# Last stage of a fused attention and MLP kernel: weight sums in the middle of Strassen groups, one set of closing products in each, and a weight split a step earlier

## Chip, cores and metric

One core of a Trainium2 chip runs the whole program. The metric is device time in microseconds (us) from start to end; the kernel before was run three times. The engines named below are TensorE (PE in the rows), VectorE (DVE), ScalarE (ACT), GpSimd (POOL) and SyncE (SP), which only issues transfers here. Each engine works through its own queue in order.

## What is computed

Attention with a window of 16 and block summaries gives x, 1536 tokens by 512. Two MLPs follow; the second is the stage of this change:

```python
def _moe_ref(x, w_in, w_out):
    h = x @ w_in
    g = h - np.tanh(h)
    return (g @ w_out).astype(np.float32)

def _moe2_ref(x, w1, w2, w3, w_out):        # d_model 512, d_ff 1024
    a = x @ w1
    b = x @ w2
    h = a * b @ w3
    return (h @ w_out).astype(np.float32)
```

All is float32.

## The kernel before

**Split arithmetic.** Each float32 operand of a matmul is held as a high part (a rounded copy, made by ScalarE) and a low part (the operand less its high part, one subtraction on GpSimd, in places on VectorE). `split_mm` (lines 185 to 188) issues three matmuls of 128x128 by 128x512: high with high, then the two mixed ones. All three add into one PSUM bank of 128x512. A matmul needs the high parts, and one of each three needs the low part of the operand that comes last.

**Stages.** The first stage is attention; beside it the product w3 w_out is formed and kept as eight tiles w34[m], so that the second MLP's last two products become one. The second stage is the first MLP. The last stage, from about 392 us of the span, is the second MLP. Its tokens are three blocks of 512 (k = 0, 1, 2), its hidden width eight chunks of 128 (m = 0 to 7).

*Block 0, steps 1 to 7* (lines 740 to 768). Step m forms a = x w1 of chunk m (`product_a`, copied by ScalarE), b = x w2 (`half`), multiplies them on VectorE (`product_b`), splits the product c into `gh_c` and `gl_c`, and then runs `final` for the chunk before: four token tiles of 128, three matmuls each, c of chunk m-1 times w34[m-1], into four banks `o`. Twelve matmuls of `final` are called a set here. `w34_split(m-1)`, ScalarE's cast `w34h` and GpSimd's subtraction `w34l`, stands in step m behind `product_a`. VectorE also decodes the weights still missing (`dec`) and, in step 4, forms sums of x (`x_sums`); in step 5 these are split (`x_split`: four casts on ScalarE, four subtractions `xl` and `t` on GpSimd).

*Blocks 1 and 2: Strassen groups* (lines 788 to 810). For a pair of chunks (m, m+1; m = 0, 2, 4, 6) and the two blocks, a group of seven products replaces eight: one group for w1, one for w2. Each product is six matmuls (`seventh`). Products 6, 5, 7 and 3 use sums of weights: `w_sums` adds high and low parts of two weight tiles (`t_w`, two full-width operations), forms two tiles `s_w` of sums (four half-width ones), all on VectorE, and then splits both on ScalarE and GpSimd. In the rows `p_w` is the bank of a product, and `t`, `xh` and `xl` are parts of x.

`group` (lines 714 to 738) is a generator. The order of its products is p1, p6, p5, p7, p2, p4, p3. Four banks take them in turn, so p2, p4 and p3 take the banks of p1, p6 and p5. ScalarE copies p1 to c11; VectorE adds the others:

```python
            tt(c21, c11, add, product(6))
            p5 = product(5)
            tt(c12, c21, add, p5)
            between()
            tt(c21, c21, add, product(7))
            tt(c22, c21, add, p5)
            yield
```

`between()` (lines 775 to 777) runs the next set of `todo`, if there is one. The w1 group's results are called `sq_a` (c11, one tile for all pairs), `a` and `ab`; the w2 group's `u_b`, `b` and `ab`. Each w2 result is multiplied into its w1 partner as soon as it is complete. `split_c` then splits the four products: those of block 1 go to `todo`, those of block 2 to `last`. The places of the weight sums: the w2 sums are made after p4 of the w1 group, the next pair's w1 sums after p4 of the w2 group, the first w1 sums at the end of step 7. Between the w1 and the w2 group `between()` is called a second time. Each pair uses up two sets of `todo`, both before its w2 group; the first pair has one.

*Closing* (lines 811 to 816). The two remaining sets of `todo`, then block 2: for each token tile j the eight chunks of `last`, three matmuls each, and the copy and the transfer out.

The order of the code is the order of each queue. Space for split weights is a list `wt.free` of places, taken from its front.

Of the kernel before, what the change touches and what calls it, by code (L numbers as in the profile page):

```python
# [19 lines left out]
P = 128  # L20
# [17 lines left out]
NM = FF2 // P  # L38
TB = 512
# [6 lines left out]
NRAW = 4  # L46
# [9 lines left out]
def fused_kernel(tc, qT, kT, vN, vW, w_in, w_out, w1, w2, w3, wo2, out):  # L56
# [128 lines left out]
    def split_mm(acc, lh, ll, rh, rl, start, stop):  # L185
        mm(out=acc, lhsT=lh, rhs=rh, start=start, stop=False)  # L186
        mm(out=acc, lhsT=lh, rhs=rl, start=False, stop=False)  # L187
        mm(out=acc, lhsT=ll, rhs=rh, start=False, stop=stop)  # L188

    def low_part(eng, out, x, high):  # L190
        eng.tensor_tensor(out=out, in0=x, in1=high.bitcast(F32), op=ALU.subtract)  # L191
# [3 lines left out]
    with tc.tile_pool(name="base", bufs=1) as base, \  # L195
# [304 lines left out]
        def bank(i, name):  # L500
            return psp.tile([P, TB], F32, tag=f"b{i}", name=name)
# [82 lines left out]
        def half(z, m, k):  # L584
            nonlocal n_ab
            ph = bank(ab[n_ab % len(ab)], f"{z}_{m}_{k}")
            n_ab += 1
            columns(ph, wt.need((z, m)), k)
            return ph
# [27 lines left out]
        for n in range(NS + LAG):  # L617
            nxt = hidden(n) if n < NS else None
            if n == NS:
                a = product_a(0, 0)  # L620
            if n == NS + 1:
                pb = half("w2", 0, 0)
            wt.start()
            if n == NS + 1:
                prev = 0, 0, product_b(0, 0, a, pb)
            wt.high()
            closing = len(evac)
            evacuate()
            cur = curve(n, nxt, cur)
            wt.low()  # L630
            if not closing:
                resplit(2)
            if n >= LAG:
                back(n - LAG)
# [10 lines left out]
        def final(m, k, c, js=range(TB // P)):  # L645
            ch, cl = c
            for j in js:
                if m == 0:
                    acc[j] = bank(outs[j], f"o_{k}_{j}")
                s = slice(j * P, (j + 1) * P)  # L650
                split_mm(acc[j], ch[:, s], cl[:, s], w34p[m][0], w34p[m][1], start=m == 0, stop=m == NM - 1)
                if m < NM - 1:
                    continue
                o = tmp(("u", "u", "gh", "gl")[j], f"out_{k}_{j}", LAG + (j > 1))
                w = DM // 2 if k == NTB - 1 and j == TB // P - 1 else DM
                for i in range(0, DM, w):
                    if j % 2 and i == 0:
                        nc.scalar.copy(out=o[:, i:i + w], in_=acc[j][:, i:i + w])
                    else:
                        nc.vector.tensor_copy(out=o[:, i:i + w], in_=acc[j][:, i:i + w])  # L660
                    nc.sync.dma_start(out=out[k * TB + j * P:k * TB + (j + 1) * P, i:i + w], in_=o[:, i:i + w])

        H = KC // 2
# [2 lines left out]
        def tt(out, in0, op, in1):  # L666
            nc.vector.tensor_tensor(out=out, in0=in0, in1=in1, op=op)  # L667

        rhs = {}

        def x_sums(c):

# [7 lines left out]
                rhs[i, c] = xh[k][:, r * H + c, :], xl[k][:, r * H + c, :], t  # L680
            rhs[6, c] = t2[0][:, :], t2[1][:, :], b22

        def x_split(i, c):
            h, l, t = rhs[i, c]
            nc.scalar.copy(out=h, in_=t)
            low_part(nc.gpsimd, l, t, h)

        def w_sums(z, m):

# [24 lines left out]
        def group(z, m, lhs, c11, c12, c21, c22):  # L714

            def product(i):
                nonlocal n_ab
                acc = bank(ab[n_ab % 4], f"p{i}_{z}_{m}")
                n_ab += 1
                seventh(acc, lhs, i)  # L720
                return acc

            nc.scalar.copy(out=c11, in_=product(1))
            tt(c21, c11, add, product(6))
            p5 = product(5)
            tt(c12, c21, add, p5)
            between()
            tt(c21, c21, add, product(7))
            tt(c22, c21, add, p5)
            yield  # L730
            tt(c11, c11, add, product(2))
            yield
            tt(c21, c21, sub, product(4))
            yield
            tt(c12, c12, add, product(3))
            wt.free.extend(lhs["places"])
            wt.release((z, m))
            wt.release((z, m + 1))

        a11 = tmp("sq", "a11")  # L740
        for m in range(1, NM):
            wt.high()
            wt.low()
            wt.start(min(2, len(wt.free) - (1 if m > 5 else (7 - m) // 2)))
            a = product_a(m, 0)
            w34_split(m - 1)
            wt.unit(1)
            pb = half("w2", m, 0)
            c = product_b(m, 0, a, pb)
            wt.unit(1)  # L750
            if m == 1:
                resplit(4)
                resplit(4)
            if m == 4:
                for i in range(H):
                    x_sums(i)
            if m == 5:
                for i in (5, 6):
                    x_split(i, 0)
                    x_split(i, 1)  # L760
                wt.free += [(px, f"x{k}{c}", f"x{k}{c + 1}", 1) for k, c in ((1, 0), (2, H))]
            if m == NM - 1:
                w34_split(m)
                assert len(wt.t) == len(wt.units)
                wt.free += [(rawp, "raw", "raw", NRAW)] * NRAW
                lhs = w_sums("w1", 0)
            final(*prev)
            prev = m, 0, c
        todo, last = [(*prev, range(TB // P))], []
        for i in (7, 4):  # L770
            x_split(i, 0)
            x_split(i, 1)
        wt.free[:0] = [(px, f"x{k}{c}", f"x{k}{c + 1}", 1) for k, c in ((2, 0), (1, H))]

        def between():
# [12 lines left out]
        for m in range(0, NM, 2):  # L788
            pl_a, a12, a21 = wt.take(f"a_{m}", F32)
            pl_b, a22, b22 = wt.take(f"ab_{m}", F32)  # L790
            g = group("w1", m, lhs, a11, a12, a21, a22)
            next(g)
            next(g)
            next(g)
            lhs = w_sums("w2", m)
            next(g, None)
            between()
            pl_c, b12, b21 = wt.take(f"b_{m}", F32)
            b11 = tmp("u", f"b11_{m}")
            g = group("w2", m, lhs, b11, b12, b21, b22)  # L800
            for a, b in ((a22, b22), (a11, b11), (a21, b21)):
                next(g)
                tt(a, a, ALU.mult, b)
            if m + 2 < NM:
                lhs = w_sums("w1", m + 2)
            next(g, None)
            tt(a12, a12, ALU.mult, b12)
            todo += [split_c(a11, m, 1), split_c(a21, m + 1, 1)]
            last += [split_c(a12, m, 2), split_c(a22, m + 1, 2)]
            wt.free += [pl_a, pl_b, pl_c]  # L810
        for i in todo:
            final(*i)
        outs = [ab[(n_ab + j) % 4] for j in range(4)]
        for j in range(TB // P):
            for i in last:
                final(*i, js=(j,))


# [48 lines left out]
```

## Time and profile before

| | us |
|---|---|
| three runs | 611.51, 613.11, 613.89 |
| median | 613.11 |
| the profiled execution | 613.43 |
| its span, first to last instruction | 611.6 |
| TensorE busy | 580.0 |
| VectorE busy | 460.3 |
| ScalarE busy | 338.6 |
| GpSimd busy | 282.1 |

Busy time counts matmuls as pipelined: a matmul's duration in the rows (0.39) is longer than the step to the next one (0.23), so the step, not the duration, tells the rate. The granted clock is a share of TensorE's 2.4 GHz, and an average over the stretch where it lies between 0.5 and 1. A name in brackets behind a row is the engine and tile that ended the idle time ahead of it.

### The profile page before, as it was taken

Reading aid. Unit: us, or ns where it says so; the run is one execution under the profiler, and the core shown is the slowest. Engines: PE = TensorE matmul, PEld = TensorE weight load, DVE = VectorE, ACT = ScalarE, POOL = GpSimd, SP = SyncE. Lnnn points to the kernel's source line nnn. Section 1 sums busy time; section 2 is a strip of 40 time slices with the busy share of each in tenths; the row PEclk is TensorE's granted clock in tenths of the full one; section 3 lists DMA queues with packets and bytes.
Section 4 is the critical chain, followed back from the end, with each engine's and each line's share of the span. In section 5 each row is a group of like instructions: output and inputs, shape, how many; then the busy total and the mean of one; then the engine's idle time right before and its main releaser. Section 6 shows DMA issues by size and latency. Waiting matters only on the chain.

```text
span 611.6 us, 9059 instructions
## 1 busy us (share of the span) xinstructions
PE 580.0 (95%) x3168; PEld 463.9 (76%) x3168; DVE 460.3 (75%) x881; ACT 338.6 (55%) x741; POOL 282.1 (46%) x237
## 2 busy tenths in 40 slices
PE   8988999998999999999999999999998989898997
PEld 6666777776888888888888888877776768676786
DVE  3789987799999987589999789996535656575710
ACT  3689987777878855567766658643234121212210
POOL 3456555555465542225646226477377151515320
PEclk9989999998999999999999999999999989898999
DMA  8889996553333210023222012230000100000021
GB/s 315 316 297 306 347 308 201 170 153 98 104 103 104 103 36 0 1 69 98 81 98 70 1 34 77 96 104 0 1 0 2 69 1 1 0 1 1 1 86 53
DMA packets 19678, 59.70 MB, mean 98 GB/s; under 512 B 2096, under 2 KB 4784, under 8 KB 19632
## 3 DMA queue, kind: packets, MB, share of 16 engines
q1 hardware_dynamic: 19632, 59.12, 29.0%
q8 instruction: 25, 0.41, 0.3%
q14 instruction: 21, 0.17, 0.1%
HBM read 54.79 MB, written 3.15 MB: 95 GB/s over the span
## 4 chain that ended last, share of the span: by engine, by line
PE 65%; DVE 15%; issue 8%; POOL 7%; ACT 3%; DMA 2%; SPq 0%; POOLq 0%; DVEq 0%; ACTq 0%
PE x L187 6%; PE x L186 6%; PE x L188 6%; PE ph L187 6%; PE ph L186 6%; PE ph L188 6%; PE o L187 3%; PE o L188 3%; PE o L186 3%; PE p_w L188 3%; PE busy L403 2%; PE p_w L186 2%; PE p_w L187 2%; DVE dec L115 2%; PE s L339 2%
## 5 line engine op out<-in xcount | busy, mean ns | idle before, releaser
L150 POOL TENSOR_TENSOR wl<-dec,wh 128x512 fp32r<-128x512 f32 x72 | 111.7, 1555 | 50.7 <-ACT wh L143 42.7
L191 POOL TENSOR_TENSOR gl<-g,gh 128x512 fp32r<-128x512 f32 x48 | 65.4, 1361 | 141.0 <-ACT gh L535 80.3
L186 PE MATMUL x<-gh,wh 128*128 128x512 f32 x192 | 75.6, 394 | 1.8 <-ACT gh L535 1.8
L187 PE MATMUL x<-gl,wh 128*128 128x512 f32 x192 | 75.4, 393 | 1.0 <-POOL gl L191 1.0
L188 PE MATMUL x<-gh,wl 128*128 128x512 f32 x192 | 75.4, 392 | 0.0
L186 PE MATMUL ph<-xh,wh 128*128 128x512 f32 x192 | 74.8, 390 | 0.0
L188 PE MATMUL ph<-xh,wl 128*128 128x512 f32 x192 | 74.7, 389 | 0.0
L187 PE MATMUL ph<-xl,wh 128*128 128x512 f32 x192 | 74.7, 389 | 0.0
L115 DVE SCALAR_TENSOR_TENSOR dec<-raw,dec 128x512 uint32<-128x512 uint32 x45 | 65.4, 1454 | 1.5
L530 ACT ACTIVATE u<-ph 128x512 f32<-128x512 f32 x48 | 28.8, 600 | 53.7 <-PE ph L188 53.7
L143 ACT CAST wh<-dec 128x512 fp32r<-128x512 f32 x72 | 44.6, 623 | 15.3 <-DVE dec L115 15.3
L191 POOL TENSOR_TENSOR s_w<-s_w,s_w 128x512 fp32r<-128x512 f32 x16 | 21.6, 1372 | 64.3 <-ACT s_w L703 56.9
L703 ACT CAST s_w<-s_w 128x512 fp32r<-128x512 f32 x16 | 9.9, 621 | 73.0 <-DVE s_w L667 72.6
L540 DVE TENSOR_TENSOR g<-ph,u 128x512 f32<-128x512 f32 x48 | 32.8, 683 | 19.5 <-ACT th L531 19.4
L186 PEld LDWEIGHTS x<-gh,wh 128*128 128x128 f32 x192 | 36.3, 189 | 10.2 <-ACT gh L535 2.2
L525 DVE COPY_PREDICATED g<-mk,th 128x512 f32<-128x512 uint32 x48 | 40.9, 853 | 4.0
L353 ACT ACTIVATE pr<-pr,nm 128x120 f32<-128x120 f32 x96 | 37.0, 390 | 12.0 <-DVE nm L350 11.7
L187 PEld LDWEIGHTS x<-gl,wh 128*128 128x128 f32 x192 | 36.5, 190 | 9.0 <-POOL gl L191 1.3
L188 PEld LDWEIGHTS x<-gh,wl 128*128 128x128 f32 x192 | 36.4, 190 | 7.6
L188 PEld LDWEIGHTS ph<-xh,wl 128*128 128x128 f32 x192 | 36.1, 188 | 7.5
L186 PEld LDWEIGHTS ph<-xh,wh 128*128 128x128 f32 x192 | 36.1, 188 | 7.5
L187 PEld LDWEIGHTS ph<-xl,wh 128*128 128x128 f32 x192 | 36.0, 188 | 7.4
(153 smaller groups left out, 1458.7 us busy)
## 6 DMA issues: line engine op xcount, KB each, us to landing
raw<-w SPq DMA_DIRECT2D x32, 512.0 KB
raw<-w_in SPq DMA_DIRECT2D x16, 512.0 KB
raw<-w_out SPq DMA_DIRECT2D x16, 512.0 KB
vg<-vW SPq DMA_DIRECT2D x8, 768.0 KB
raw<-wo SPq DMA_DIRECT2D x8, 512.0 KB
kt<-kT SPq DMA_DIRECT2D x7, 544.0 KB
vn<-vN SPq DMA_DIRECT2D x8, 384.0 KB
qt<-qT SPq DMA_DIRECT2D x7, 384.0 KB
```

The lines of the kernel that those rows point to most:

```text
L115: lambda tu=tu, su=su, lo=lo: stt(out=tu, in0=lo, scalar=29, in1=su, op0=ALU.logical_shift_right, op1=ALU.bitwise_or)])
L143: nc.scalar.copy(out=h, in_=self.t[n])
L150: nc.gpsimd.tensor_tensor(out=l, in0=self.t[self.n_low], in1=h[:, :].bitcast(F32), op=ALU.subtract)
L186: mm(out=acc, lhsT=lh, rhs=rh, start=start, stop=False)
L187: mm(out=acc, lhsT=lh, rhs=rl, start=False, stop=False)
L188: mm(out=acc, lhsT=ll, rhs=rh, start=False, stop=stop)
L191: eng.tensor_tensor(out=out, in0=x, in1=high.bitcast(F32), op=ALU.subtract)
L339: mm(out=ps[r, i, :], lhsT=qt[n][r, t * QT:(t + 1) * QT], rhs=kt[n][r, t * CW:t * CW + NC], start=True, stop=True)
L353: nc.scalar.activation(out=pr[g][:, i, :], in_=pr[g][:, i, :], func=AF.Exp, scale=-1.0, bias=nm[g][:, i:i + 1], accum_out=z[g][:, i:i + 1])
L525: nc.vector.copy_predicated(out=g, mask=mask[:, :].bitcast(U32), data=t)
L530: nc.scalar.activation(out=u, in_=ph, func=AF.Square)
L540: nc.vector.tensor_tensor(out=gn, in0=ph, in1=u, op=ALU.mult)
```

## The change

Five things.

1. `group` gains a `yield` behind the sum with p5. The w2 sums are made there, in the w1 group; the next pair's w1 sums there, in the w2 group.
2. The second `between()` is gone. The set in the middle of the w2 group, which found `todo` empty before, now takes one: one set in each group. The first pair's w2 group still finds none.
3. `w34_split(m)` stands at the end of step m, ahead of `final` of the chunk before; `w34_split(0)` one step further forward, in the last step of the stage before. The number of places that `wt.start` leaves free is lowered to suit.
4. In step 5 the four subtractions of `x_split` go from GpSimd to VectorE. In step 7 the first w1 sums stand ahead of `product_a`.
5. At the end, token tile 0 of block 2 is run for six of its eight chunks ahead of the two remaining sets, in banks of its own (`spare`).

```
                 pb = half("w2", 0, 0)
+                w34_split(0)
...
-                    acc[j] = bank(outs[j], f"o_{k}_{j}")
+                    acc[k, j] = bank((outs + spare)[j + TB // P * (k == 2)], f"o_{k}_{j}")
...
-        def x_split(i, c):
+        def x_split(i, c, eng):
             h, l, t = rhs[i, c]
             nc.scalar.copy(out=h, in_=t)
-            low_part(nc.gpsimd, l, t, h)
+            low_part(eng, l, t, h)
...
             tt(c12, c21, add, p5)
+            yield
             between()
...
-            wt.start(min(2, len(wt.free) - (1 if m > 5 else (7 - m) // 2)))
+            wt.start(min(2, len(wt.free) - (1 if m > 5 else (6 - m) // 2)))
+            if m == NM - 1:
+                assert len(wt.t) == len(wt.units)
+                wt.free += [(rawp, "raw", "raw", NRAW)] * NRAW
+                lhs = w_sums("w1", 0)
             a = product_a(m, 0)
-            w34_split(m - 1)
...
-                    x_split(i, 0)
-                    x_split(i, 1)
+                    x_split(i, 0, nc.vector)
+                    x_split(i, 1, nc.vector)
...
-            if m == NM - 1:
-                w34_split(m)
-                assert len(wt.t) == len(wt.units)
-                wt.free += [(rawp, "raw", "raw", NRAW)] * NRAW
-                lhs = w_sums("w1", 0)
+            w34_split(m)
             final(*prev)
...
             next(g)
-            next(g)
-            next(g)
             lhs = w_sums("w2", m)
-            next(g, None)
-            between()
+            for _ in range(4):
+                next(g, None)
...
             g = group("w2", m, lhs, b11, b12, b21, b22)
+            next(g)
+            if m + 2 < NM:
+                lhs = w_sums("w1", m + 2)
             for a, b in ((a22, b22), (a11, b11), (a21, b21)):
                 next(g)
                 tt(a, a, ALU.mult, b)
-            if m + 2 < NM:
-                lhs = w_sums("w1", m + 2)
...
+        spare += [ab[(n_ab + j) % 4] for j in range(4)]
+        for i in last[:NM - 2]:
+            final(*i, js=(0,))
         for i in todo:
             final(*i)
-        outs = [ab[(n_ab + j) % 4] for j in range(4)]
         for j in range(TB // P):
-            for i in last:
+            for i in last[0 if j else NM - 2:]:
```

What the order of the queues shows at three places. First GpSimd in steps 4 to 6 of block 0 (`gl_c` is the low part of c, `xl` and `t` are the x splits). Before:

```order
L191 TENSOR_TENSOR w34l_4791<-w_4_113,w34h_0_4789 128x512
L191 TENSOR_TENSOR gl_c_0_4809<-u_a_0_4787,gh_c_0_4808 128x512
L191 TENSOR_TENSOR xl_122<-x2a_0_1976,xh_119 128x512
L191 TENSOR_TENSOR xl_122<-x2a_1_1977,xh_119 128x512
L191 TENSOR_TENSOR t_1_0_4755<-x2a_2_1982,t_0_0_4754 128x512
L191 TENSOR_TENSOR t_1_1_4761<-x2a_3_1983,t_0_1_4760 128x512
L191 TENSOR_TENSOR w34l_4849<-w_5_114,w34h_1_4790 128x512
```

GpSimd in the same steps, after:

```order
L191 TENSOR_TENSOR w34l_4764<-w_4_113,w34h_0_4762 128x512
L191 TENSOR_TENSOR gl_c_0_4809<-u_a_0_4792,gh_c_0_4808 128x512
L191 TENSOR_TENSOR w34l_4820<-w_5_114,w34h_1_4763 128x512
L191 TENSOR_TENSOR gl_c_0_4870<-u_a_0_4850,gh_c_0_4869 128x512
L191 TENSOR_TENSOR w34l_4875<-w_6_115,w34h_0_4873 128x512
L150 TENSOR_TENSOR wl_4891<-dec_4835,wh_4890 128x512
```

The low part of w34[5] now follows c of chunk 5 at once, and the four splits are no longer ahead of it.

Then VectorE in the w2 group of the second pair, from the sum with p5 on (bank `p_w_2_5287` before, `p_w_2_5275` after). Before:

```order
L667 TENSOR_TENSOR b_0_5268<-b_1_5269,p_w_2_5287 128x512
L667 TENSOR_TENSOR b_1_5269<-b_1_5269,p_w_2_5295 128x512
L667 TENSOR_TENSOR ab_1_5164<-b_1_5269,p_w_2_5287 128x512
L667 TENSOR_TENSOR ab_0_5163<-ab_0_5163,ab_1_5164 128x512
L667 TENSOR_TENSOR u_b_2_5270<-u_b_2_5270,p_w_2_5305 128x512
L667 TENSOR_TENSOR sq_a_4513<-sq_a_4513,u_b_2_5270 128x512
L667 TENSOR_TENSOR b_1_5269<-b_1_5269,p_w_2_5314 128x512
L667 TENSOR_TENSOR a_5162<-a_5162,b_1_5269 128x512
L667 TENSOR_TENSOR t_w_4_5323<-wh_4444,wl_4445 128x512
L667 TENSOR_TENSOR t_w_4_5324<-wh_4514,wl_4515 128x512
L667 TENSOR_TENSOR s_w_4_5325<-t_w_4_5324 128x256
```

VectorE there, after:

```order
L668 TENSOR_TENSOR b_0_5256<-b_1_5257,p_w_2_5275 128x512
L668 TENSOR_TENSOR t_w_4_5283<-wh_4444,wl_4445 128x512
L668 TENSOR_TENSOR t_w_4_5284<-wh_4519,wl_4520 128x512
L668 TENSOR_TENSOR s_w_4_5285<-t_w_4_5284 128x256
L668 TENSOR_TENSOR s_w_4_5285<-s_w_4_5285,t_w_4_5283 128x256
L668 TENSOR_TENSOR s_w_4_5286<-t_w_4_5283,t_w_4_5284 128x256
L668 TENSOR_TENSOR s_w_4_5286<-t_w_4_5283,s_w_4_5285 128x256
L668 TENSOR_TENSOR b_1_5257<-b_1_5257,p_w_2_5311 128x512
L668 TENSOR_TENSOR ab_1_5164<-b_1_5257,p_w_2_5275 128x512
```

The six weight sums move from behind the product with p4 to behind the first use of p5's bank, and ahead of its second use (`ab_1`).

Last TensorE in the same group, at the end of p5. Before:

```order
L186 MATMUL p_w_2_5287<-xh_119,s_w_2_5_0_5240 128x512
L187 MATMUL p_w_2_5287<-xl_122,s_w_2_5_0_5240 128x512
L188 MATMUL p_w_2_5287<-xh_119,s_w_2_5_1_5241 128x512
L186 MATMUL p_w_2_5295<-xh_117,s_w_2_7_0_5244 128x512
L187 MATMUL p_w_2_5295<-xl_120,s_w_2_7_0_5244 128x512
```

TensorE there, after:

```order
L188 MATMUL p_w_2_5275<-xh_119,s_w_2_5_1_5200 128x512
L186 MATMUL o_0_5207<-w34h_1_4482,gh_c_1_5151 128x512
L187 MATMUL o_0_5207<-w34l_4574,gh_c_1_5151 128x512
L188 MATMUL o_0_5207<-w34h_1_4482,gl_c_1_5152 128x512
L186 MATMUL o_1_5211<-w34h_1_4482,gh_c_1_5151 128x512
L187 MATMUL o_1_5211<-w34l_4574,gh_c_1_5151 128x512
```

A set of twelve now stands between p5 and p7 of this group; before, it stood ahead of the group's p1.

## Rows read from the trace of the kernel before

**Rows 1.** Page, busy time of TensorE: us, share of the span, instructions.
```profile
PE 580.0 (95%) x3168; PEld 463.9 (76%) x3168; DVE 460.3 (75%) x881; ACT 338.6 (55%) x741; POOL 282.1 (46%) x237
```
**Rows 2.** Waits of PE, 440 to 612: us in total, times, longest.
```profile
PE p_w L186 <- ACT s_w L703: 9.2, 5, 2.4
PE p_w L188 <- POOL s_w L191: 2.5, 4, 0.6
```
**Rows 3.** Timeline of PE, six marks: start, duration, engine, line, operation.
```profile
406.76 0.50 PE L186 MATMUL o<-w34h,gh_c 128*128 128x512 f32 x1
...
463.34 0.40 PE L186 MATMUL p_w<-xh,wh 128*128 128x512 f32 x1
...
528.30 0.40 PE L186 MATMUL o<-w34h,gh_c 128*128 128x512 f32 x1
...
549.95 0.39 PE L188 MATMUL p_w<-xh,wl 128*128 128x512 f32 x1
...
578.81 0.50 PE L186 MATMUL o<-w34h,gh_c 128*128 128x512 f32 x1
...
607.67 0.40 PE L188 MATMUL o<-w34h,c 128*128 128x512 f32 x1
```
**Rows 4.** Timeline of PE, matmuls that waited: idle before them and its releaser.
```profile
408.55 0.50 PE L187 MATMUL o<-sq_w34l,gh_c 128*128 128x512 f32 x1 [1.28 <-POOL sq_w34l L191]
...
466.30 0.51 PE L186 MATMUL p_w<-t,s_w 128*128 128x512 f32 x1 [1.42 <-ACT s_w L703]
...
552.67 0.51 PE L186 MATMUL p_w<-t,s_w 128*128 128x512 f32 x1 [2.34 <-ACT s_w L703]
...
554.03 0.58 PE L188 MATMUL p_w<-t,s_w 128*128 128x512 f32 x1 [0.62 <-POOL s_w L191]
...
580.61 0.51 PE L188 MATMUL o<-w34h,gl_c 128*128 128x512 f32 x1 [1.07 <-POOL gl_c L191]
```
**Rows 5.** Stretches: us, busy PE, PEld, DVE, ACT, POOL, granted clock, DMA, GB/s.
```profile
463.00:470.00 7.00, 4.96 (x21) 3.44 (x20) 3.23 (x4) 3.80 (x7) 5.99 (x5) 1.00 0.00 1
...
491.00:499.80 8.80, 5.77 (x18) 3.99 (x17) 5.49 (x10) 4.00 (x7) 5.92 (x5) 0.81 0.01 2
...
520.80:527.00 6.20, 3.83 (x10) 2.31 (x9) 4.46 (x8) 3.42 (x6) 3.39 (x3) 0.73 0.00 0
...
549.80:557.70 7.90, 4.94 (x14) 3.33 (x13) 4.71 (x9) 4.00 (x7) 5.00 (x4) 0.79 0.00 1
```
**Rows 6.** Timeline of DVE around the end of the third pair's w2 group.
```profile
544.93 0.69 DVE L667 TENSOR_TENSOR b<-b,p_w 128x512 f32<-128x512 f32 x1 [0.70 <-PE p_w L188]
...
549.63 0.68 DVE L667 TENSOR_TENSOR t_w<-wh,wl 128x512 f32<-128x512 f32 x1
...
552.16 0.42 DVE L667 TENSOR_TENSOR s_w<-t_w,s_w 128x256 f32<-128x256 f32 x1
552.50 0.68 DVE L667 TENSOR_TENSOR b<-b,p_w 128x512 f32<-128x512 f32 x1
553.21 1.31 DVE L667 TENSOR_TENSOR a<-a,b 128x512 f32<-128x512 f32 x1
```
**Rows 7.** Timelines of ACT and POOL at the same place.
```profile
552.00 1.29 ACT L703 CAST s_w<-s_w 128x512 fp32r<-128x512 f32 x2 [10.65 <-DVE s_w L667]
...
556.93 0.58 ACT L723 COPY sq_a<-p_w 128x512 f32<-128x512 f32 x1 [1.23 <-POOL gl_c L191]
...
552.70 2.97 POOL L191 TENSOR_TENSOR s_w<-s_w,s_w 128x512 fp32r<-128x512 f32 x2 [11.15 <-ACT s_w L703]
```
**Rows 8.** Timelines of POOL and DVE in step 7, and the first group.
```profile
462.27 1.62 POOL L191 TENSOR_TENSOR gl_c<-u_a,gh_c 128x512 fp32r<-128x512 f32 x1 [1.79 <-ACT gh_c L600]
...
468.82 5.04 POOL L191 TENSOR_TENSOR xl<-x2a,xh 128x512 fp32r<-128x512 f32 x4
...
462.78 1.39 DVE L667 TENSOR_TENSOR s_w<-t_w 128x256 f32<-128x256 f32 x1
464.21 1.39 DVE L667 TENSOR_TENSOR s_w<-s_w,t_w 128x256 f32<-128x256 f32 x1
```

More of the change, by code (lines that the diff above doesn't have):

```diff
@@ L648, in final @@
                 if m == 0:
-                    acc[j] = bank(outs[j], f"o_{k}_{j}")
+                    acc[k, j] = bank((outs + spare)[j + TB // P * (k == 2)], f"o_{k}_{j}")
                 s = slice(j * P, (j + 1) * P)
-                split_mm(acc[j], ch[:, s], cl[:, s], w34p[m][0], w34p[m][1], start=m == 0, stop=m == NM - 1)
+                split_mm(acc[k, j], ch[:, s], cl[:, s], w34p[m][0], w34p[m][1], start=m == 0, stop=m == NM - 1)
                 if m < NM - 1:
@@ L657, in final @@
                     if j % 2 and i == 0:
-                        nc.scalar.copy(out=o[:, i:i + w], in_=acc[j][:, i:i + w])
+                        nc.scalar.copy(out=o[:, i:i + w], in_=acc[k, j][:, i:i + w])
                     else:
-                        nc.vector.tensor_copy(out=o[:, i:i + w], in_=acc[j][:, i:i + w])
+                        nc.vector.tensor_copy(out=o[:, i:i + w], in_=acc[k, j][:, i:i + w])
                     nc.sync.dma_start(out=out[k * TB + j * P:k * TB + (j + 1) * P, i:i + w], in_=o[:, i:i + w])
@@ L667, in tt @@
             nc.vector.tensor_tensor(out=out, in0=in0, in1=in1, op=op)
-        rhs = {}
+        rhs, spare = {}, []
         def x_sums(c):
@@ L770, in fused_kernel @@
         for i in (7, 4):
-            x_split(i, 0)
-            x_split(i, 1)
+            x_split(i, 0, nc.gpsimd)
+            x_split(i, 1, nc.gpsimd)
         wt.free[:0] = [(px, f"x{k}{c}", f"x{k}{c + 1}", 1) for k, c in ((2, 0), (1, H))]
```

## The prediction

> **What bounds the kernel now.** The page's busy times come first: TensorE is busy 95% of the span, no other engine over 76% [rows 1], so the time is TensorE's own work plus what it waits. The view of waits, cut to the last third, names for whom: the first product that takes a sum of weights waits five times for ScalarE's high part of it, 9.2 us in all, and then four times for GpSimd's low part, 2.5 [rows 2].
>
> To price the waits I count matmuls. From the first matmul of an `o` product at 528.30 to the last of p1 at 549.95 lie 95 steps without a wait: 21.65 / 95 = 0.228 us each [rows 3]. So one Strassen product (6 matmuls) takes 1.37 and one set of w3 w_out products (12, `final` in the code) 2.73. Three stretches stand against that [rows 3]. **A**, 406.76 to 463.34, the plain steps: 228 matmuls are 52.0, measured 56.6, so 4.6 over. **B**, 463.34 to 578.81, the Strassen groups: 420 matmuls (56 products and 7 sets) are 95.7, measured 115.5, so 19.8 over. **C**, 578.81 to 607.67, the closing sets: 119 are 27.1, measured 28.9, so 1.7 over. Together 26.1.
>
> Where they sit: in A at the second matmul of a set, which needs the low part of w34 (idle 1.28 at 408.55, and four smaller or like it); in B at p6 of a w1 group (1.42 at 466.30; 2.34 and 0.62 at 552.67 and 554.03); in C once, at 580.61 [rows 4]. B's 19.8 is more than the 11.7 of idle time in [rows 2]. Three of the five waits, those before w1 groups 2, 4 and 6, are followed by a lower clock: in the stretches from 491, 520.8 and 549.8 the granted clock is 0.81, 0.73 and 0.79, a mixture of 2.4 and 1.2 GHz, which is worth at most 0.19 x 8.8, 0.27 x 6.2 and 0.21 x 7.9, each time 1.7 [rows 5]. After the shorter waits around 466.30 the clock stayed at 1.00 [rows 5].
>
> Why p6 waits: VectorE forms the six weight sums of the next w1 group only after p4 of the w2 group has been added, 549.63 to 552.50; then come ScalarE's cast (552.00) and GpSimd's low part (552.70), and TensorE has only p1 to do meanwhile [rows 6, 7].
>
> **The change part by part.**
> *Weight sums in the middle of a group.* They now stand on VectorE right behind the sum with p5. From there to the next group's p6, TensorE has a set (2.73), p7, p2, p4, p3 and p1: 2.73 + 5 x 1.37 = 9.6. The chain needs 0.7 for the p5 sum, some 2.3 until the first half is summed (549.63 to 551.9), 0.7 for the cast and 1.3 for the low part: 5.0 [rows 6, 7]. Where there is no set (the w2 group of the first pair) the cover is 6.8. All five waits at p6 go, and the low clock with them. The sums for the very first w1 group move ahead of step 7's products in the same way. Gain: B's 19.8.
>
> *w34 split a step ahead.* One cast and one subtraction move half a step forward per step; GpSimd did the subtraction behind `wl` and, in step 5, behind four splits of x sums. These four go to VectorE: 2.8 at the price of its sums, ahead of the decoding of a weight that step 7 is the first to use. The low part is then done a step before its set. Gain: A's 4.6. No DMA changes its place.
>
> *End.* Six quarter sets (18 matmuls, 4.1) of finished parts stand ahead of the sets that wait for GpSimd's last splits. Gain: about C's 1.7. The spare banks belong to p7 and its followers, read by then.
>
> So without any new wait: 613.43 (the profiled execution; the median of three is 613.11) - 26.1 = **587.3**.
>
> *What is late next.* The sums now stand ahead of VectorE's additions of p7 and of p5 into c22, and c22 is what frees p5's bank, which p3 takes. Let T be the end of p5. VectorE: sum with p5 0.7, weight sums 2.87, two dependent additions 1.4, so c22 is done at T + 5.0 [rows 6]. TensorE comes to p3 at T + 3 x 1.37 = 4.1 without a set between, at 6.8 with one.
> (a) w2 group, first pair, no set: waits 0.9, whatever else happens.
> (b) w2 groups of the other three pairs: VectorE is on time at p5, 1.8 to spare: 0.
> (c) w1 groups of pairs 2, 4, 6: VectorE is late here. From the end E of the w2 group's p3 it still has products to finish: nine operations of 0.67 (seven from 544.93 to 549.63) from p7's end, E - 4.1, are done at E + 1.9, and one or two of them stand beside a GpSimd subtraction and double (1.31 at 553.21, where a sum takes 0.68) [rows 6]: E + 3.2. Then ScalarE has two casts and the copy of p1 into `sq_a` (as at 556.93, behind GpSimd's use of that tile), about 1.8 [rows 7]; VectorE two sums, 1.4; the weight sums 2.87; two additions, 1.4: E + 10.7 with no other delay. TensorE reaches p3 at E + 4.1 + 2.7 + 4.1 = 10.9. So nothing to spare, and the four splits of c on GpSimd fall just there: one subtraction in the way is up to 1.3 more [rows 8]. I take 1.0 each for pairs 4 and 6, and 1.9 for pair 2, where (a) leaves VectorE about 0.9 later: 3.9, between 0 and 7.
> (d) w1 group, first pair: VectorE has two output copies more (1.3 at the price of sums) and GpSimd's four x splits (5.04) lie beside the weight sums [rows 8]: c22 at T + 6.3 to T + 8.4 against 6.8; I take 1.2, between 0 and 1.6.
> (e) step 7: the weight sums now stand beside three GpSimd subtractions, the third the low part of the last w2 unit, which TensorE needs 0.5 into the next product: 0.4, between 0 and 0.8.
> Sum 0.9 + 3.9 + 1.2 + 0.4 = 6.4, and 0.1 at each restart (0.5): 587.3 + 6.9 = **594.2**. Each of these waits is under 2 us, like those after which the clock stayed at 1.00, so I add nothing for it.
>
> The price of meeting GpSimd is read from step 7 of the kernel before: two half-width sums, 0.42 elsewhere, took 1.39 each, the first beside a subtraction that began at 462.27 [rows 6, 8]. The Trainium skill (SBUF — State Buffer, Who interferes with whom) states that a VectorE instruction with two SBUF inputs contends with a GpSimd one that reads SBUF, and that the later one blocks fully. By that, the sums placed in the middle of groups would meet whatever GpSimd does there, which speaks against the new place. The rows agree.
>
> **The rivals.**
> 1. *Cover holds everywhere but in (a).* For: (c) is a tie before any collision. Against: four GpSimd splits follow each pair. 587.3 + 0.9 = 588.2.
> 2. *VectorE and GpSimd meet in every group.* The weight sums then take 2.87 + 2 x 0.97 = 4.8, as in step 7 [rows 8]. Waits at p3: (a) 2.8; (c) 3.8 + 2.9 + 2.9; (d) 2.8; (b) 3 x 0.1; (e) 0.8: 16.3, so 603.6; with four waits long enough to bring the low clock, at 1.7 each, 610. The rule of the Trainium skill named above (SBUF — State Buffer, Who interferes with whom) is this rival's mechanism. Against: in the w2 groups GpSimd is idle until the sums themselves feed it.
> 3. *Slower: VectorE becomes the bound.* Place: p3 of all eight groups. Per pair VectorE has 14 sums and 4 products of 0.7 and two times 2.87, 18.3, against TensorE's 84 + 24 matmuls, 24.6. GpSimd has eight subtractions a pair of 1.26 [rows 8]; if every one blocks VectorE for its whole length that is 28.4. Over four pairs 15, and the low clock after each of eight waits, 1.7 each, 14: 587.3 + 29 = 616. It is slower than before from 26.1 / 8 = 3.3 us per group on. Against: it needs every collision, each at full length, and a wait in each group long enough for the clock.
> 4. *The split a step ahead does not come early*, since the cast still queues behind ScalarE's copies: A's 4.6 stays: 598.8. Against: the cast follows the c cast directly, and its subtraction is needed 5 us later.
>
> **How the numbers follow.** Forecast 594.2: 0.58. Rival 1: 0.18. Rival 2: 0.13. Rival 4: 0.06. Rival 3: 0.03; the last 0.02 is something else on the no-change side. The range reaches below to rival 1 less the 1.2 by which the three runs spread to either side: 587. Above, (c), (d) and (e) at their upper bounds give 587.3 + 0.9 + 7 + 1.6 + 0.8 + 0.5 = 598.1, rival 4 598.8; to leave no more than 2 in 10 out it takes in rival 2 without the low clock: 604. A measurement of this kernel tells about 0.5% (3.1 us) from no change: of the cases above, rival 2 with the low clock (0.02 of its 0.13) and the last 0.02 lie within it, rival 3 is slower. Faster 0.93, same 0.04, slower 0.03.
>
> **What would show it.** Right: no wait of p6 for ScalarE's `s_w`; no wait for `w34l`; granted clock 1.00 from 405 us on; TensorE's waits, if any, at p3 for VectorE, largest in the w2 group of the first pair and the w1 group of the second; about 31 us from the first closing matmul to the end of the span (now 32.8). Wrong: waits at p6 that stay (the sums come late all the same), waits at p3 over 2.3 us with a clock below 1.00 behind them, or waits at p7 or at the sets for GpSimd's splits, which I hold hidden.

## The result and the profile after

| | before | after |
|---|---|---|
| median, us | 613.5 (611.51 to 616.28) | **593.15** (592.24 to 600.07) |
| profiled execution, us | 613.43 | 592.24 |
| its span, us | 611.6 | 590.4 |
| last stage in it, us | 390.23 to 607.67: 217.44 | 389.90 to 586.47: 196.57 |

Four runs each; the ratio is 0.969 with an interval of 0.9607 to 0.9773, which is wide because one of the four runs of after took 600.07. The forecast was 594.2.

"Last stage" is the stretch from the first matmul of a `w` product to the last matmul of the kernel. It is what the change touches, and it holds 20.87 of the 21.19 us between the two profiled executions. The moment at which it begins differs by up to 3 us from execution to execution, so single executions are compared below by its length. What it would last without any wait is 217.44 less the 26.1 of the prediction, 191.3; what a kernel has above that is called its excess.

The busy times of after's page, with engine, us, share of the span and instructions (to be laid beside [rows 1]), and then the waits of PE from 390 to 592 us, in total, times, longest (beside [rows 2]):
```profile
PE 571.6 (97%) x3168; PEld 461.4 (78%) x3168; DVE 465.4 (79%) x885; ACT 338.6 (57%) x741; POOL 278.9 (47%) x233
```
```profile
PE p_w L186 <- DVE ab L668: 3.2, 3, 1.4
PE w L188 <- POOL wl L150: 0.2, 1, 0.2
```
The waits of [rows 2] for `s_w` are gone, those for `w34l` and for `gl_c` too. Three waits have come, of a product for VectorE's `ab`, the tile that holds c22. In the timeline of PE (start, duration, engine, line, operation, idle before it and its releaser; beside [rows 3, 4]) these are the four matmuls of the last stage that waited for over 0.1 us, and, in the last two rows, the first and the last matmul of the closing sets, which waited for nothing:
```profile
453.29 0.50 PE L188 MATMUL w<-xh,wl 128*128 128x512 f32 x1 [0.18 <-POOL wl L150]
...
470.63 0.50 PE L186 MATMUL p_w<-xh,s_w 128*128 128x512 f32 x1 [0.90 <-DVE ab L668]
...
481.41 0.50 PE L186 MATMUL p_w<-xh,s_w 128*128 128x512 f32 x1 [0.87 <-DVE ab L668]
...
495.42 0.50 PE L186 MATMUL p_w<-xh,s_w 128*128 128x512 f32 x1 [1.38 <-DVE ab L668]
...
559.05 0.40 PE L186 MATMUL o<-w34h,c 128*128 128x512 f32 x1
...
586.47 0.40 PE L188 MATMUL o<-w34h,c 128*128 128x512 f32 x1
```
All three are p3, in the w1 and the w2 group of the first pair and in the w1 group of the second. The stretches of after (columns as in [rows 5]: busy time of PE, PEld, DVE, ACT, POOL, then the granted clock, the share of the DMA engines and GB/s) have full clock throughout, where [rows 5] had 0.81, 0.73 and 0.79:
```profile
450.00:480.00 30.00, 28.92 (x125) 23.01 (x124) 18.03 (x29) 8.84 (x16) 15.87 (x13) 1.00 0.10 36
480.00:500.00 20.00, 17.75 (x77) 13.95 (x76) 15.15 (x24) 5.34 (x10) 11.01 (x8) 1.00 0.00 1
500.00:560.00 60.00, 60.00 (x263) 48.80 (x262) 43.38 (x70) 12.60 (x22) 22.85 (x17) 1.00 0.00 1
```
In VectorE's timeline the p3 waits end with the addition into c22, the `ab` at 494.68 that follows the two `t_w` (now right behind the additions of p5) by way of the half sums into `s_w`:
```profile
490.67 1.72 DVE L668 TENSOR_TENSOR t_w<-wh,wl 128x512 f32<-128x512 f32 x2
...
494.68 0.69 DVE L668 TENSOR_TENSOR ab<-a,p_w 128x512 f32<-128x512 f32 x1
```
It ends at 495.37, and p3 starts at 495.42.

### The profile page after: what moved, and what is told of

Its sections match the earlier page's. It is cut to its first block, busy times and chain, and to the rows that moved or that the text cites. A ratio compares the mean times of both kernels' runs of the same rounds, so it can differ in the third digit from the quotient of the medians.

```text
span 590.4 us, 9062 instructions
## 1 busy us (share of the span) xinstructions
PE 571.6 (97%) x3168; PEld 461.4 (78%) x3168; DVE 465.4 (79%) x885; ACT 338.6 (57%) x741; POOL 278.9 (47%) x233
## 4 chain that ended last, share of the span: by engine, by line
PE 76%; DVE 14%; issue 6%; POOL 2%; ACT 1%; DMA 1%; DVEq 0%; POOLq 0%; ACTq 0%
PE x L187 6%; PE x L188 6%; PE x L186 6%; PE ph L187 6%; PE ph L188 6%; PE ph L186 6%; PE p_w L186 3%; PE p_w L187 3%; PE p_w L188 3%; PE o L188 3%; PE o L186 3%; PE o L187 3%; PE s L339 2%; PE busy L403 2%; PE w L188 2%
## 5 line engine op out<-in xcount | busy, mean ns | idle before, releaser
L115 DVE SCALAR_TENSOR_TENSOR dec<-raw,dec 128x512 uint32<-128x512 uint32 x45 | 62.4, 1387 | 1.5
L540 DVE TENSOR_TENSOR g<-ph,u 128x512 f32<-128x512 f32 x48 | 32.7, 682 | 19.8 <-ACT th L531 19.8
L542 DVE SCALAR_TENSOR_TENSOR g<-sq,g 128x512 f32<-128x512 f32 x48 | 40.3, 839 | 0.7 <-ACT sq L538 0.6
L191 POOL TENSOR_TENSOR s_w<-s_w,s_w 128x512 fp32r<-128x512 f32 x16 | 20.4, 1292 | 38.9 <-ACT s_w L704 36.0
```

What stands on the lines that cost most here:

```text
L115: lambda tu=tu, su=su, lo=lo: stt(out=tu, in0=lo, scalar=29, in1=su, op0=ALU.logical_shift_right, op1=ALU.bitwise_or)])
L540: nc.vector.tensor_tensor(out=gn, in0=ph, in1=u, op=ALU.mult)
L542: nc.vector.scalar_tensor_tensor(out=gn, in0=sq, scalar=GAM, in1=gn, op0=ALU.add, op1=ALU.mult)
```

## Experiments

**The theory.** (1) The waits at p6 and their low clock are gone because the sums of weights begin right behind p5, with a set behind them as cover. (2) What is left at p3 is p5's bank, held until c22, because the weight sums stand ahead of it on VectorE. (3) Where p3 is late in the first pair, GpSimd's splits stretch the sums. **The rivals:** for (2), VectorE is late with everything, so that freeing the bank earlier only moves the wait to the next bank; for (1), the set alone is the cover and the place of the sums does little, or the gain is mostly the clock's; for (3), VectorE has too many operations there, whoever runs beside it.

The ten kernels all compute the whole result, and six of them were run once. Waits that an edit does not reach repeat closely from run to run: p3 of the first pair's w2 group lies 1.03 or 1.04 over the step, its restart not counted, in all eight traces that have this wait. All are made from the kernel after, except that `sums_only` and `split_only` are before with a part of the change.

### p5's bank freed without c21: `c22_p7`

c12 already holds c21 + p5, so c22 = c12 + p7, and p5 is not read a second time.
```
-            tt(c21, c21, add, product(7))
-            tt(c22, c21, add, p5)
+            p7 = product(7)
+            tt(c21, c21, add, p7)
+            tt(c22, c12, add, p7)
```


> The changed kernel, but c22 is formed as c12 + p7 instead of c21 + p5 (c12 is c21 + p5 at that moment, so the sum is the same). p5's bank is then free after VectorE's first addition, ahead of the weight sums; p7's bank is held instead until c22. Theory (p3 waits for p5's bank, which the weight sums hold up): the three waits of TensorE at p3 (1.16 + 1.14 + 1.65 us with their restarts in the trace of the changed kernel) go, and the next user of p7's bank, p1 of the next group, comes late enough: 592.2 - 3.9 = 588.3 us. Rival (VectorE as a whole is late, the bank is only where it shows): the waits move to p1 of the next group or to p2, and the time stays within 1 us of 592.2.

Measured: 588.97 median of four (587.04 to 590.63), ratio to before 0.9604 (0.9578 to 0.963); last stage 192.80, 3.77 less than after. The waits of PE in the last stage:
```profile
PE p_w L186 <- DVE ab L668: 0.2, 1, 0.2
PE w L188 <- POOL wl L150: 0.2, 1, 0.2
```
The three p3 waits of after together cost 3.95 over the step (the table below, in the section on the prediction); the change of one operand removes them. VectorE has as many operations as in after (885), and no later bank is waited for, except 0.2 at 493.53, p1 of the second pair's w2 group:
```profile
493.53 0.50 PE L186 MATMUL p_w<-xh,wh 128*128 128x512 f32 x1 [0.23 <-DVE ab L668]
```
So (2) holds: it was the bank, not the load of VectorE.

### One half of the change alone: `sums_only` and `split_only`

`sums_only` is before with the sums in the middle of the groups and one set in each; `split_only` is before with w34 split a step ahead and four splits of step 5 on VectorE. `sums_only` keeps the w34 split, the four splits on GpSimd, the first sums at the end of step 7 and the old end; `split_only` keeps the place of the sums and sets, and the old end. Against after, their cores are:
```
sums_only:
-                w34_split(0)
...
-                lhs = w_sums("w1", 0)
...
             a = product_a(m, 0)
+            w34_split(m - 1)
...
-                    x_split(i, 0, nc.vector)
-                    x_split(i, 1, nc.vector)
+                    x_split(i, 0)
+                    x_split(i, 1)
...
-            w34_split(m)
+            if m == NM - 1:
+                w34_split(m)
...
+                lhs = w_sums("w1", 0)
             final(*prev)
...
-        for i in last[:NM - 2]:
-            final(*i, js=(0,))
...
-            for i in last[0 if j else NM - 2:]:
+            for i in last:
split_only:
-            yield
             between()
...
-                lhs = w_sums("w1", 0)
             a = product_a(m, 0)
...
+                lhs = w_sums("w1", 0)
             final(*prev)
...
+            next(g)
+            next(g)
             lhs = w_sums("w2", m)
-            for _ in range(4):
-                next(g, None)
+            next(g, None)
+            between()
...
-            next(g)
-            if m + 2 < NM:
-                lhs = w_sums("w1", m + 2)
...
+            if m + 2 < NM:
+                lhs = w_sums("w1", m + 2)
...
-        for i in last[:NM - 2]:
-            final(*i, js=(0,))
...
-            for i in last[0 if j else NM - 2:]:
+            for i in last:
```


> The kernel before with the first two parts alone: the weight sums in the middle of a group and one set in each group. The split of w34, the first w1 sums and the end stay as they were. Theory: of the 26.1 us over, the waits in A (4.6), the first wait at p6 (2.6) and the end (1.7) stay; those at p6 of the w2 group of the first pair (2.0) and of the w1 groups 2, 4, 6 (5.2, 4.4, 5.1) go, and the waits at p3 come (3.9): 613.1 - 16.7 + 3.9 = 600.3 us. Rival (the moved sums need the other parts to pay, since what is late is passed on): above 604.

> The kernel before with the split of w34 half a step ahead and the four subtractions of step 5 on VectorE, nothing else. Theory: the waits at the sets of the plain steps go and nothing else moves: 613.1 - 4.6 = 608.5 us, with B and C of the kernel before unchanged (19.8 and 1.7 over). Rival: TensorE, 4.6 us earlier, meets the first weight sums that much later, so that the first wait at p6 grows and the gain is under 2 us.

`sums_only`: 601.89 (600.99 to 603.2), ratio 0.9823 (0.9801 to 0.9845); last stage 206.44, 11.0 less than before. `split_only`: 609.62 (607.0 to 614.42, ten runs), ratio 0.9928 (0.9889 to 0.9967); last stage 213.82, 3.6 less. The waits of PE in the last stage of `sums_only`, then of `split_only`:
```profile
PE p_w L186 <- DVE ab L667: 2.8, 3, 1.4
PE o L187 <- POOL w34l L191: 1.6, 2, 1.4
PE p_w L186 <- ACT s_w L703: 1.4, 1, 1.4
PE o L187 <- POOL sq_w34l L191: 1.3, 1, 1.3
PE o L188 <- POOL gl_c L191: 1.1, 1, 1.1
PE p_w L188 <- POOL s_w L191: 0.6, 1, 0.6
```
```profile
PE p_w L186 <- ACT s_w L704: 9.2, 5, 2.4
PE p_w L188 <- POOL s_w L191: 2.9, 5, 0.6
PE o L188 <- POOL gl_c L191: 1.1, 1, 1.1
```
Each part removes its own waits and leaves the other's: the sums take away four of the five p6 waits and bring three at p3, the split takes away every wait for w34. In `split_only` the first wait at p6 does not grow (1.55 and 0.80 over the step, 1.58 and 0.79 in before). Both kernels are above what was expected, by 1.6 and by 1.1, and the place of that is the clock. In `sums_only` the same short wait at p6 that before has with full clock is followed by a lower one. The stretch around it in `sums_only`, and then in before:
```profile
464.00:471.00 7.00, 5.55 (x16) 4.18 (x17) 1.82 (x5) 3.80 (x7) 6.15 (x5) 0.76 0.00 1
```
```profile
465.50:472.00 6.50, 5.08 (x21) 3.85 (x22) 1.38 (x4) 4.08 (x8) 5.68 (x5) 1.00 0.00 1
```
In `split_only` the low clock behind the second pair's wait lasts longer than in before, where [rows 5] has 0.81:
```profile
488.00:497.00 9.00, 7.68 (x20) 5.74 (x21) 3.96 (x7) 4.00 (x7) 7.92 (x6) 0.62 0.01 2
```
Counted in matmuls at 0.228, it costs 2.8 there, where before had 1.6. What decides whether the clock falls, and for how long, isn't shown by the wait alone.

### One group put back: `late_one`

The sums of w1 group 4 alone are formed behind p4 again.
```
-            if m + 2 < NM:
+            if m + 2 < NM and m != 2:
                 lhs = w_sums("w1", m + 2)
...
+            if m == 2:
+                lhs = w_sums("w1", m + 2)
```


> The changed kernel, but the w1 sums of pair 4 alone are made where they were before, after p4 of pair 2's w2 group. Theory (such a wait costs its idle time and a low clock behind it): p6 of that w1 group waits about 2.4 for ScalarE and 0.6 for GpSimd, the granted clock falls below 0.9 in the stretch behind, and the place costs 4.4 to 5.2: 592.2 + 4.8 = 597.0. Rival (the idle time alone): 3.4, 595.6, with the clock at 1.00.

Measured: 597.68 in one execution; last stage 202.65, 6.08 more than after. The waits at p6 are back in that one group (PE's timeline), and the clock with them (a stretch):
```profile
512.51 0.50 PE L186 MATMUL p_w<-t,s_w 128*128 128x512 f32 x1 [2.23 <-ACT s_w L704]
...
513.88 0.79 PE L188 MATMUL p_w<-t,s_w 128*128 128x512 f32 x1 [0.57 <-POOL s_w L191]
514.47 0.63 PE L186 MATMUL p_w<-t,s_w 128*128 128x512 f32 x1
514.90 0.63 PE L187 MATMUL p_w<-t,s_w 128*128 128x512 f32 x1
```
```profile
511.00:521.00 10.00, 7.92 (x21) 5.95 (x22) 6.44 (x10) 4.01 (x7) 8.45 (x6) 0.66 0.00 0
```
The waits are 2.38 + 0.80 over the step, the low clock 2.8 more; the last two rows lie 0.43 apart, near twice the step, as at 1.2 GHz. That is more than the 4.4 to 5.2 expected, which had the low clock at the 1.6 of before. The set in the middle of pair 2's w2 group is still there, so a set alone does not cover sums that come late, and the clock is less than half of the price. The place of the sums is worth 6.1 us for this group. Counted in the same way, the five waits of before cost 2.6, 2.0, 5.2, 4.4 and 5.1, together 19.3 of B's 19.8.

### Two sets in a row: `two_sets`

In the three later pairs the second set stands behind the whole w1 group, and none is left for the middle of the w2 group.
```
             for _ in range(4):
                 next(g, None)
+            between()
             pl_c, b12, b21 = wt.take(f"b_{m}", F32)
```


> The changed kernel with the second between() put back: both sets of a pair stand around the w1 group, none in the w2 group. The weight sums stay where the change put them. Theory (a set behind p5 is what covers the weight sums): p3 of the w2 groups of pairs 2 and 4 now waits like that of the first pair, 1.1 each, and p3 of the w1 groups 4 and 6 like that of group 2, 1.65 each, so 5.5 more than the changed kernel's 592.2: 597.7 us. Rival (the place of the sums alone does it, the set's place is indifferent): 592.2 within 1.

Measured: 595.65 in one execution that reached the last stage early (387.98); last stage 201.92, 5.35 more than after, where 5.5 was expected. The waits of PE:
```profile
PE p_w L186 <- DVE ab L668: 7.6, 7, 1.4
PE w L188 <- POOL wl L150: 0.2, 1, 0.2
```
All groups that form sums for a next one, seven, wait at p3, 1.0 to 1.6 each over the step, and none at p6. A w1 group waits too, though it has its set: VectorE comes late out of the w2 group's wait, as in the second pair of after. So the middle of a group is early enough for p6 even without a set behind p5; what that set covers is p3.

### GpSimd taken out of the first group: `xs4_vector`
```
         for i in (7, 4):
-            x_split(i, 0, nc.gpsimd)
-            x_split(i, 1, nc.gpsimd)
+            x_split(i, 0, nc.vector)
+            x_split(i, 1, nc.vector)
```


> The changed kernel with the last four x splits (products 7 and 4) on VectorE instead of GpSimd. Theory (in the first w1 group the weight sums meet GpSimd's splits, first two of them 2.22 instead of 1.29 us, and c21 waits for the splits): the first p3 wait, 1.16, goes, the others stay: 591.1 us. Rival (two output copies and VectorE's own load cause that wait): VectorE has 2.8 us more to do, the wait stays or grows, 592.2 or more.

Measured: 592.12 in one execution that reached the last stage late (391.01); last stage 195.37, 1.20 less than after (1.16 expected). The first p3 wait is gone, the other two are as they were. The pair of `t_w` sums in that group in after, beside GpSimd's four splits, and then in `xs4_vector`:
```profile
464.18 2.22 DVE L668 TENSOR_TENSOR t_w<-wh,wl 128x512 f32<-128x512 f32 x2
...
460.19 5.06 POOL L191 TENSOR_TENSOR xl<-x2a,xh 128x512 fp32r<-128x512 f32 x4
```
```profile
464.84 1.29 DVE L668 TENSOR_TENSOR t_w<-wh,wl 128x512 f32<-128x512 f32 x2
```
VectorE does four operations more and is still in time, so (3) holds in its main part: GpSimd's splits, not the number of VectorE's operations, made that wait. But stretching the sums is only one of two ways in which they did. VectorE's first addition of the group, c21, is free to go when p6 is done, about 461.5 in after, and stands until the second of the four splits is done, because `a` takes the place in memory that this split reads (`wt.free`):
```profile
462.78 0.69 DVE L668 TENSOR_TENSOR a<-sq_a,p_w 128x512 f32<-128x512 f32 x1 [5.82 <-POOL xl L191]
```
Counted from the group's first matmul, c22 is done 1.4 earlier in `xs4_vector`: 0.9 by the shorter sums and 0.4 because they begin earlier.

### The end put back: `no_end`
```
-        for i in last[:NM - 2]:
-            final(*i, js=(0,))
...
-            for i in last[0 if j else NM - 2:]:
+            for i in last:
```


> The changed kernel without its last part: the remaining sets of todo come first, block 2 behind them, as before. Theory: the wait at the third matmul of the first closing set is there again, 1.2, with 0.3 of restarts, and nothing else changes: 592.2 + 1.5 = 593.7 us. Rival (the splits of c are early now that VectorE is not late): no wait, 592.2.

Measured: 593.15 in one execution; last stage 198.20, 1.63 more than after (1.5 expected), with the old wait for `gl_c`:
```profile
PE o L188 <- POOL gl_c L191: 1.1, 1, 1.1
```

### The first sums late again: `first_late`
```
-                lhs = w_sums("w1", 0)
             a = product_a(m, 0)
...
             w34_split(m)
+            if m == NM - 1:
+                lhs = w_sums("w1", 0)
```


> The changed kernel, but the very first w1 sums are made at the end of step 7 again, behind the products. Theory: the wait of 0.45 for wl goes and the first p6 waits for ScalarE and GpSimd as before, 1.6 + 0.8 and 0.2 of restarts, 2.6: the last stage (first w matmul to last matmul, 196.6 us in the changed kernel) becomes 198.7. If the low clock follows this wait, as it did in the kernel with the moved sums alone and did not in the kernel before, 1.6 more: 200.3. Rival (the place of the first sums is indifferent): 196.6.

Measured: 597.2 in one execution; last stage 201.51, 4.94 more than after, above both expectations. The p6 wait is back (1.55 + 0.80), with full clock, and the wait for `wl` is gone; but the p3 wait of the group has grown to 2.28, since the late sums push GpSimd's x splits back and VectorE's c21 stands behind them as in after, and it is that one which is followed by a low clock. The stretches at p6 and at p3:
```profile
460.50:467.00 6.50, 5.34 (x22) 4.07 (x23) 1.27 (x4) 3.66 (x7) 5.95 (x5) 1.00 0.00 1
...
473.00:480.50 7.50, 6.52 (x21) 5.19 (x22) 3.09 (x6) 0.60 (x2) 0.91 (x1) 0.77 0.35 131
```
What both expectations missed is that one late step makes the next one late too.

### Step 5's splits back on GpSimd: `xs_gpsimd`
```
                 for i in (5, 6):
-                    x_split(i, 0, nc.vector)
-                    x_split(i, 1, nc.vector)
+                    x_split(i, 0, nc.gpsimd)
+                    x_split(i, 1, nc.gpsimd)
```


> The changed kernel with the four x splits of step 5 on GpSimd again. Theory: the split of w34 a step ahead is enough by itself but for one set; w34l of chunk 5 stands behind four subtractions (5.1 us) and is ready some 0.8 late for its set in step 6: the last stage is 197.5 us against 196.6. Rival 1 (VectorE's relief in step 5 pays for more than that, since the weight's decoding comes 4 us earlier and the wait for wl goes): 196.2 or less. Rival 2 (the four splits were the whole of the wait in step 6, 1.6): 198.2.

Measured: 593.9 in one execution; last stage 197.94, 1.37 more than after (0.9 expected: 0.8 for the wait). The part with the split a step ahead needs this move: without it the low part of w34 comes too late by
```profile
PE o L187 <- POOL w34l L191: 1.8, 1, 1.8
```
since it stands behind four splits. GpSimd's timeline has the first two at 1.27 each; the other two and the low part itself run beside VectorE's work, the decoding of a weight and then the first weight sums, and take 1.59 and 1.71:
```profile
442.10 2.54 POOL L191 TENSOR_TENSOR xl<-x2a,xh 128x512 fp32r<-128x512 f32 x2
444.60 3.17 POOL L191 TENSOR_TENSOR t<-x2a,t 128x512 fp32r<-128x512 f32 x2
447.73 1.71 POOL L191 TENSOR_TENSOR w34l<-w,w34h 128x512 fp32r<-128x512 f32 x1
```
The wait costs 2.1 with its restart, more than twice what was expected. The net is smaller because, as the first rival said, the wait for `wl` goes (0.45), and the first p3 wait is 0.27 shorter.

### Both p5's bank and `wl`: `wl_first`

`c22_p7`, and in step 6 the last weight's low part ahead of the w34 split.
```
+            if m == NM - 2:
+                wt.high()
+                wt.low()
             w34_split(m)
```


> The kernel with c22 = c12 + p7, and in step 6 the split of the last weight (wh, wl) ahead of that of w34[6]. Theory (of the two waits left in that kernel, the one for wl comes from wl standing third on GpSimd beside the first weight sums): that wait, 0.45 with its restart, goes, the 0.38 at p1 of the second pair's w2 group stays: 0.45 under the 588.7 of the profiled execution of that kernel, 588.3. Rival: w34l, now a place later, makes its set wait, or GpSimd meets VectorE elsewhere: 588.7 or more.

Measured: 587.39 median of four (585.88 to 588.54), ratio to before 0.9596 (0.9569 to 0.9622); last stage 192.32, 0.48 less than `c22_p7`. The wait for `wl` is gone from the trace, and one of 0.2 is left in the whole last stage. Between `c22_p7` and `wl_first` the timed runs, on two chips, overlap; only the trace tells them apart. Against after's 593.15 this is the best version found.

The excess over 191.3 of each kernel, from its last stage, puts them side by side:

| kernel | last stage | excess |
|---|---|---|
| before | 217.44 | 26.1 |
| `split_only` | 213.82 | 22.5 |
| `sums_only` | 206.44 | 15.1 |
| `late_one` | 202.65 | 11.3 |
| `two_sets` | 201.92 | 10.6 |
| `first_late` | 201.51 | 10.2 |
| `no_end` | 198.20 | 6.9 |
| `xs_gpsimd` | 197.94 | 6.6 |
| after | 196.57 | 5.3 |
| `xs4_vector` | 195.37 | 4.1 |
| `c22_p7` | 192.80 | 1.5 |
| `wl_first` | 192.32 | 1.0 |

## Why the prediction was right, step by step

**The floor.** 26.1 us of waits and low clock were to go. Without a wait the time was to be 587.3, and `wl_first`, which has next to none, takes 587.39. That the totals agree to 0.1 is luck, since its profiled execution reached the last stage 1.4 earlier than before's; by length, its last stage is 1.0 over the 191.3 that were counted. The count of matmuls at one step each, made where nothing waits, is what carried this.

**A, B and C** are all gone from after's trace. Undone one by one they come back, in whole or in part: the w34 splits (1.37 in `xs_gpsimd`; done alone, in `split_only`, the move gains 3.6 of 4.6, and the longer low clock there takes back about 1), one group's sums (6.08 in `late_one`), the closing sets (1.63 in `no_end`, 1.7 predicted). From the first closing matmul at 559.05 to the end of the span are 31.35, 31 predicted.

**The new waits**, over the step of 0.228 and with the restart:

| term | predicted | measured |
|---|---|---|
| (a) w2 group, first pair | 0.9 + 0.1 | 1.14 |
| (b) other w2 groups | 0 | 0 |
| (c) w1 group, second pair | 1.9 + 0.1 | 1.65 |
| (c) w1 groups, third and fourth pair | 1.0 + 1.0, + 0.2 | 0.04 + 0.11 |
| (d) w1 group, first pair | 1.2 + 0.1 | 1.16 |
| (e) `wl` in step 7 | 0.4 + 0.1 | 0.45 |

All stand at the place and for the engine that was named. The size of (d) is right, but its working lacks a step: it put the lateness down to two output copies and stretched sums, while about 0.7 of it stands ahead of the sums, where c21 waits for GpSimd's second split (`xs4_vector`). **The mis-sized term is (c) of the last two pairs**: 2.2 was put there, 0.15 measured. The working gave a tie, c22 done at E + 10.7 and p3 at E + 10.9, and 1 us was added for a GpSimd subtraction in the way. In the third pair's w1 group of after, VectorE's c22 ends at 519.50 + 0.69 = 520.19 and p3 starts at 520.31 without an idle time:
```profile
519.50 0.69 DVE L668 TENSOR_TENSOR ab<-a,p_w 128x512 f32<-128x512 f32 x1
```
```profile
520.31 0.44 PE L186 MATMUL p_w<-xh,s_w 128*128 128x512 f32 x1
```
With E, the start of this group's p1, at 509.33, that is E + 10.9 and E + 11.0: the tie was there, 0.1 apart, and it stayed on the right side by little. The subtraction is in the way, but it costs less than was added: the pair of `t_w` takes 1.73 (at 515.49) beside GpSimd's `c` split (514.78 for 1.28), 0.44 more than the 1.29 of `xs4_vector`, and the steps ahead of the sums were done about 0.3 sooner than worked out:
```profile
515.49 1.73 DVE L668 TENSOR_TENSOR t_w<-wh,wl 128x512 f32<-128x512 f32 x2
```
```profile
514.78 1.28 POOL L191 TENSOR_TENSOR c<-ab,c 128x512 fp32r<-128x512 f32 x1
```
Only the part of the subtraction that was still running when the sums began, 0.57, could count. With the measured terms the sum is 587.3 + 4.6 = 591.9, against 592.24 in the profiled execution; 0.3 of the difference between the two kernels lies outside the last stage.

**The rivals.** Rival 1 (588.2) was right for the last two pairs only. Rival 2 needed long sums in every group: the pair of `t_w` took 2.22 in the first, 1.28 or 1.29 in the w2 groups and 1.72 or 1.73 in the other w1 groups, a part of what it assumed. Its mechanism is real where a GpSimd subtraction is still running when the sums begin, in the w1 groups. The Trainium skill (SBUF — State Buffer, Who interferes with whom) states that a VectorE operation with two SBUF inputs and a GpSimd operation that reads SBUF hold each other up. The trace agrees in the first group, where the two `t_w` sums went from 2.22 in after to 1.29 in `xs4_vector`. Rivals 3 and 4 found no row.

**A step that held here without being a rule.** The prediction added nothing for low clock, since its waits were under 2 us like those after which the clock stayed at 1.00. It did stay in after. But a wait of 1.58 + 0.78 over the step at the first p6 was followed by 0.76 in `sums_only` and by 1.00 in before, and 1.55 + 0.80 by 1.00 in `split_only` and `first_late`. The reason given was not enough; that the clock stayed at 1.00 in after isn't explained by it, and this step held by luck as far as the runs tell.

## What to carry to other kernels

Price waits by counting matmuls at the step that a stretch without waits shows, since the list of waits leaves out the low clock behind them (11.7 us of idle time stood for 19.8 here). When side work is moved ahead of a step, ask which buffer that step releases and who takes it next; then look for another operand that gives the same result and releases it earlier (c22 from c12 and p7: 3.8 us). Where a working gives a tie, price a collision by the part of the other operation that is still running, not by its whole length (here 0.57 was left of a subtraction of 1.28, and the sums took 0.44 longer). And when a new tile takes the place of an old one, ask who reads the old one last: c21 of the first group stood behind a split for that reason.

## What the runs showed of the hardware

The price of a low clock varied more than the waits before it. Behind a p6 wait of about 2.4 us it cost 1.6 in before and 2.8 in `split_only` (both in the second pair), and 2.8 in `late_one`, each counted in matmuls over the step. Behind one of 1.6 + 0.8 it was nothing in three kernels (before, `split_only`, `first_late`) and about 1.6 in a fourth (`sums_only`). The stretches behind them have a granted clock of 0.62 to 0.81, a mixture of 2.4 and 1.2 GHz; in `late_one` the matmuls at 514.47 and 514.90 lie 0.43 apart, near twice the step, so what differs between the kernels is how long the lower level lasts. What sets that stays open: in no run was the work ahead of a wait varied by itself.
